# A recurrent attention and maxout kernel: k and v of the first step move to the ScalarE DMA queue

## The chip, the cores and the metric

The kernel runs on one core of a Trainium2 chip. The metric is the device time of one execution in microseconds. A core has five engines that run beside one another and wait for one another by semaphores: TensorE (PE), VectorE (DVE), ScalarE (ACT), GpSimd (POOL) and SyncE (SP). SyncE and ScalarE each have a queue on which they issue DMAs.

## The reference

```
state = alpha[t, :, None] * state + outer(k[t], v[t])     # for each of 4 batches x 8 heads, head width 48
y[t]  = q[t] @ state                                      # t = 0 .. 767
x     = y laid out as 3072 tokens x 384
out   = max(x @ w1, x @ w2, x @ w3) @ w_out               # 384 -> 768 -> 384
```

The inputs q, k, v and alpha are float32 of shape (4, 8, 768, 48), the output is float32, 3072 x 384.

## The kernel before

The sequence is cut into six blocks of 128 positions, and the batches into two pairs; one step is one block of one pair (16 heads), so there are twelve steps. Step s works on block s // 2. Within a block, the recurrence is done as masked attention, after k and q have been scaled by cumulated decays. Between blocks a state is carried.

Each step loads four tiles of 128 positions x 16 heads x 48 values in float32, named ra (alpha), rk, rq and rv; each is one DMA of 384 KB whose rows are 192 bytes. The function `load` (lines 81 to 87) issues them in the order alpha, k, q, v, all on the SyncE queue, and each kind of tile has four buffers. Two constants are loaded on the ScalarE queue: c16 (line 92, 128 x 386 in float16, the triangle, the identity, the mask and a small weight, c_68 in the profile) and c32 (line 93, 128 x 6 in float32, biases and scales of ScalarE's activations, c_69 in the profile). In the program `load(0)` comes first, then the two constants, then `load(1)` and `load(2)`, the twelve loads of weights (lines 120 and 125), `load(3)` and `load(4)`. Later loads are issued one per step. Ahead of everything, ScalarE loads its table of functions (line 72). On each queue the DMAs are issued in program order.

The order of the compute work is written out by hand, in strings of pieces such as `D0@1` (piece D, half 0, step 1), and each engine takes its part of them in that order. The prologue starts with

```
N0@0 H11@0 D0@0 D1@0 H9@0 N0@1 V0@0 T0@0 T1@0 A0@0 A1@0 D0@1 Y0@0 D1@1 T0@1 N0@2 ...
```

- N (`logs`, line 137): ScalarE takes the logarithm of alpha. Its output is a tile la.
- H (`warm`, line 296): TensorE multiplies a blank tile, 512 columns at a time, 11 times or 9 times here. Nothing reads the result.
- D (`decays`, lines 146 to 163): TensorE multiplies the triangle in c16 with the logarithms (L146) and gathers sums (L149). ScalarE takes two exponentials with biases from c32 (ic at L155, ac at L156). VectorE (GpSimd from step 3 on) multiplies k by ic and q by ac (L159, L160).
- V (`values`, line 170): ScalarE scales v with a column of c32. Its output is vt.
- T (`turn`, lines 179 and 183): TensorE transposes the scaled q and k with the identity in c16, VectorE copies them out.
- A (`scores`, lines 193 and 196): scores on TensorE, masked on VectorE.
- Y (`attend`, lines 207 to 214): the attention output on TensorE, copied out by ScalarE (xb, L214). X (`turn_back`, lines 222 and 225) transposes it for the second part.
- W casts weights on GpSimd (L130), M and S carry the state (L233 to L254), G (L268) and O (L285) are the matmuls of the second part.

TensorE, ScalarE and VectorE all work in order, so an instruction that waits holds up what is behind it on its engine. After the prologue, a string FIRST does the second part for steps 0 and 1, and from step 2 on each step runs the attention of a later step beside the second part of an earlier one.

Of the kernel before, what the change touches and what calls it, by code (L numbers as in the profile page):

```python
# [23 lines left out]
def kernel(  # L24
# [12 lines left out]
    nc = tc.nc  # L37
# [40 lines left out]
    def where(s):  # L78
        return s // (B // U), (s % (B // U)) * U

    def load(s):
        cb, b0 = where(s)
        for n in ("a", "k", "q", "v"):
            t = raw.tile([P, NH, D], FP32, name=f"r{n}", tag=f"r{n}")
            nc.sync.dma_start(  # L85
                t, ins[n][cb * P:(cb + 1) * P, b0:b0 + U].rearrange("s b h d -> s (b h) d"))
            raws[s, n] = t

    c16 = cpool.tile([P, 3 * P + 2], FP16, name="c16")
    c32 = cpool.tile([P, 6], FP32, name="c32")  # L90
    load(0)
    nc.scalar.dma_start(c16, nc.inline_tensor(c16_np, name="c16").ap())
    nc.scalar.dma_start(c32, nc.inline_tensor(c32_np, name="c32").ap())
# [240 lines left out]
    LAST = """G0 G1 G2 G3 G4 G5 G6 G7 O1 G8 O0"""  # L334

    load(1)
    load(2)
    load_weights()
    load(3)
# [43 lines left out]
```

## Time and profile before

| What | us |
|---|---|
| time before, median of 2 runs | 171.71 |
| the two runs | 170.89 and 172.54 |
| span of the profiled execution, first to last instruction | 168.8 |
| the median above that span | 2.9 |
| TensorE (matmul) busy, share of the span | 156.9, 93% |
| VectorE busy | 112.2, 66% |
| ScalarE busy | 99.0, 59% |
| GpSimd busy | 49.0, 29% |

For the profiled execution only its span is recorded; how far its own time lies above that isn't recorded apart, so the median stands for it. Times in the profile count from the span's start. In the list of DMA issues, the last number is the time from the issue to the landing of the data. SPq and ACTq are the DMA queues of SyncE and ScalarE, and a busy entry on them is the time that the issue took. The rows with digits cut the span into 40 slices of about 4.2 us, and a 9 means 90% busy or more. In a table of stretches the columns are the stretch, its length, the busy time and count of PE, PEld (the loading of weights into TensorE), DVE, ACT and POOL, the clock granted to TensorE, the mean busy share of the 16 DMA engines (over 1 when their packets overlap), and GB/s.

### The profile page before, as it was taken

What the parts mean: (1) busy time and instruction counts of PE and PEld (TensorE: products, weight loads), DVE (VectorE), ACT (ScalarE), POOL (GpSimd) and SP (SyncE); (2) the same over time, 40 slices, a digit from 0 to 9 for tenths busy, and PEclk for the clock granted to TensorE, in tenths of its full rate; (3) what the DMA queues carried; (4) which work ended last, traced back from release to release, by engine and by line L of the source; (5) the groups of instructions that cost most, each with busy time, mean ns of one, the idle gap of its engine ahead of it and who ended that gap; (6) DMA issues with size and microseconds to landing.
All of it is one profiled execution on the core that took longest, in us unless ns stands there. A gap on an engine that the chain in (4) does not pass through costs nothing.

```text
span 168.8 us, 4329 instructions
## 1 busy us (share of the span) xinstructions
PE 156.9 (93%) x1758; PEld 121.1 (72%) x1758; DVE 112.2 (66%) x185; ACT 99.0 (59%) x181; POOL 49.0 (29%) x72
## 2 busy tenths in 40 slices
PE   7955859999999999999999999999999999999992
PEld 2423637699887676886877978968968869869860
DVE  4186777756647757597587587687667775975730
ACT  3616585142777684874974964956856748435232
POOL 0000005756063454404512531541442244100000
PEclk9995675599999999999999999999999999999999
DMA  6999999998999999999897967948931011020013
GB/s 131 223 219 218 176 247 336 355 360 170 226 172 213 218 248 254 192 226 221 219 223 189 235 105 177 228 91 192 212 92 50 0 56 41 0 93 4 0 47 140
DMA packets 107251, 28.68 MB, mean 170 GB/s; under 512 B 99808, under 2 KB 107232, under 8 KB 107232
## 3 DMA queue, kind: packets, MB, share of 16 engines
q1 hardware_dynamic: 106944, 28.32, 77.3%
q8 instruction: 13, 0.21, 0.6%
q10 hardware_dynamic: 288, 0.10, 0.3%
q14 instruction: 6, 0.05, 0.1%
HBM read 23.69 MB, written 4.72 MB: 168 GB/s over the span
## 4 chain that ended last, share of the span: by engine, by line
PE 81%; SPq 7%; DMA 3%; ACT 3%; DVE 2%; issue 1%; ACTq 0%
PE ops L285 14%; SPq L85 7%; PE tps L179 6%; DMA ra<-in_alpha_dram 3%; PE yps L210 3%; PE xtp L222 2%; PE lps L146 2%; PE yps L207 2%; PE sps L250 2%; PE sps L247 2%; DVE lat L196 1%; PE lps L149 1%; ACT xb L214 1%; PE gps_514 L268 1%; PE gps_523 L268 1%
## 5 line engine op out<-in xcount | busy, mean ns | idle before, releaser
L268 PEld LDWEIGHTS <-wcat 128*128 128x128 f16 x648 | 60.3, 98 | 9.0 <-POOL gm L235 0.2
L285 PE MATMUL ops<-wo_97,hT 128*128 128x384 f16 x144 | 27.1, 327 | 0.0
L288 ACT COPY ob<-ops 128x384 f32<-128x384 f32 x24 | 11.5, 480 | 14.2 <-PE ops L285 14.2
L155 ACT ACTIVATE ic<-lps,c_69 128x384 f32<-128x384 f32 x24 | 13.9, 581 | 8.4 <-PE lps L146 5.1
L285 PEld LDWEIGHTS <-hT 128*128 128x128 f16 x144 | 12.8, 98 | 7.5
L183 DVE COPY qkT<-tps 128x1024 f16<-128x1024 f16 x24 | 16.4, 683 | 1.3 <-PE tps L179 1.1
L214 ACT ACTIVATE xb<-yps,c_69 128x384 f16<-128x384 f32 x24 | 14.0, 585 | 4.8 <-PE yps L210 4.8
L156 ACT ACTIVATE ac<-lps,c_69 128x384 f32<-128x384 f32 x24 | 13.8, 575 | 0.0
L210 PE MATMUL yps<-vt,lat 128*128 128x48 f16 x192 | 12.2, 190 | 0.6 <-ACT vt L170 0.6
L193 PEld LDWEIGHTS <-qkT 48*128 48x128 f16 x192 | 6.3, 98 | 8.8 <-issue 7.7
L159 POOL TENSOR_TENSOR qk_87<-rk,ic 128x384 f16<-128x384 f32 x6 | 6.0, 997 | 21.9 <-ACT ic L155 21.9
L210 PEld LDWEIGHTS <-lat 128*128 128x128 f16 x192 | 10.5, 101 | 1.5 <-DVE lat L196 0.7
L170 ACT ACTIVATE vt<-rv,c_69 128x768 f16<-128x768 f32 x12 | 11.3, 940 | 0.0
L225 ACT COPY xT<-xtp 128x768 f16<-128x768 f16 x12 | 9.6, 803 | 1.0 <-PE xtp L222 1.0
L296 PE MATMUL wps<-blank 128*128 128x512 f16 x22 | 8.0, 528 | 1.2 <-DVE blank L343 1.2
L159 POOL TENSOR_TENSOR qk_86<-rk,ic 128x384 f16<-128x384 f32 x4 | 4.0, 997 | 15.4 <-ACT ic L155 15.4
L130 POOL CAST wcat<-ws_0_114 128x768 f16<-128x768 f32 x1 | 0.8, 823 | 26.3 <-DMA ws_0_114<-in_moe_w_dram 26.3
L159 POOL TENSOR_TENSOR qk_85<-rk,ic 128x384 f16<-128x384 f32 x4 | 4.0, 995 | 13.9 <-ACT ic L155 13.9
L207 PEld LDWEIGHTS <-qkT 128*128 128x128 f16 x80 | 7.7, 98 | 0.4
L222 PE MATMUL xtp<-c_68,xb 128*128 128x128 f16 x72 | 7.4, 228 | 0.5 <-ACT xb L214 0.3
L159 POOL TENSOR_TENSOR qk_84<-rk,ic 128x384 f16<-128x384 f32 x4 | 4.0, 996 | 12.4 <-ACT ic L155 12.4
L222 PEld LDWEIGHTS <-xb 128*128 128x128 f16 x72 | 5.2, 101 | 2.3 <-ACT xb L214 0.9
(409 smaller groups left out, 359.6 us busy)
## 6 DMA issues: line engine op xcount, KB each, us to landing
ra<-in_alpha_dram SPq DMA_DIRECT2D x12, 384.0 KB, 4.7
rk<-in_k_dram SPq DMA_DIRECT2D x12, 384.0 KB, 5.6
rq<-in_q_dram SPq DMA_DIRECT2D x12, 384.0 KB, 5.8
rv<-in_v_dram SPq DMA_DIRECT2D x12, 384.0 KB, 5.7
out_dram<-ob SPq DMA_DIRECT2D x24, 192.0 KB, 2.0
ws_0_114<-in_moe_w_dram SPq DMA_DIRECT2D x1, 384.0 KB, 4.9
ws_1_116<-in_moe_w_dram SPq DMA_DIRECT2D x1, 384.0 KB, 4.5
ws_2_118<-in_moe_w_dram SPq DMA_DIRECT2D x1, 384.0 KB, 5.0
```

The lines of the kernel that those rows point to most:

```text
L85: nc.sync.dma_start(t, ins[n][cb * P:(cb + 1) * P, b0:b0 + U].rearrange("s b h d -> s (b h) d"))
L155: nc.scalar.activation(out=ic, in_=lv, func=AFT.Exp, bias=nat_c, scale=-1.0)
L156: nc.scalar.activation(out=ac, in_=lv, func=AFT.Exp, bias=at_c)
L159: eng.tensor_mul(kv, raws[s, "k"][:, hs], ic)
L170: nc.scalar.mul(vt, raws.pop((s, "v")), vs_c)
L183: nc.vector.tensor_copy(out=qkT, in_=tps)
L210: nc.tensor.matmul(yps[:, p, i, :], lat[:, i, p, :], vt[:, u * H + 2 * p + i, :], start=(cb == 0), stop=(cb == 0 or i == 1))
L214: nc.scalar.mul(xb, yps.rearrange("p a b d -> p (a b d)"), ys_c)
L222: nc.tensor.transpose(xtp[:, u, f, :], xb[:, f * P:(f + 1) * P], ident)
L268: nc.tensor.matmul(gps[:, j, :], wcat[:, f, g, jj * P:(jj + 1) * P], xT[:, f].rearrange("p u t -> p (u t)"), start=(f == 0), stop=(f == NF ...
L285: nc.tensor.matmul(ops, hT_of[s][:, jj, u * P:(u + 1) * P], wo16[:, jj, :], start=(jj == 0), stop=(jj == NJ - 1))
L288: nc.scalar.copy(out=ob, in_=ops)
```

## The change

In step 0, and only there, the loads of k and v are issued on the ScalarE queue. Alpha and q stay on SyncE's. The program order of the four loads and of the constants is unchanged, so ScalarE's queue now holds k, v, c16, c32 and SyncE's holds alpha and q of step 0, then alpha, k, q, v of step 1, and so on. No other instruction moves on any engine.

```
         for n in ("a", "k", "q", "v"):
             t = raw.tile([P, NH, D], FP32, name=f"r{n}", tag=f"r{n}")
-            nc.sync.dma_start(
+            queue = nc.scalar if s == 0 and n in "kv" else nc.sync
+            queue.dma_start(
                 t, ins[n][cb * P:(cb + 1) * P, b0:b0 + U].rearrange("s b h d -> s (b h) d"))
             raws[s, n] = t
```

More of the change, by code (lines that the diff above doesn't have):

```diff
@@ L84, in load @@
             t = raw.tile([P, NH, D], FP32, name=f"r{n}", tag=f"r{n}")
-            nc.sync.dma_start(
+            queue = nc.scalar if s == 0 and n in "kv" else nc.sync
+            queue.dma_start(
                 t, ins[n][cb * P:(cb + 1) * P, b0:b0 + U].rearrange("s b h d -> s (b h) d"))
```

## The prediction

> **What bounds the kernel now.** I read the page first, then the timeline of the first 24 us, the DMA issues with their times to landing, the stretches of 2 us, and the chain that ended last. The page says that TensorE sets the time once it is running:
>
> ```profile
> span 168.8 us, 4329 instructions
> PE   7955859999999999999999999999999999999992
> DMA  6999999998999999999897967948931011020013
> PE 81%; SPq 7%; DMA 3%; ACT 3%; DVE 2%; issue 1%; ACTq 0%
> ```
>
> TensorE is full from slice 8 (about 30 us) to the end; before that it has gaps, and the DMA engines are full from slice 2 to 11. So the change, which touches only the loads of step 0, works in the first 30 us, and what it delays there comes out at the end one for one, unless a gap in the first 30 us takes it up. The timeline of that start:
>
> ```profile
> 0.74 0.43 SPq L85 DMA_DIRECT2D ra<-in_alpha_dram  x1
> 0.77 0.40 ACTq L92 DMA_DIRECT2D c_68<-c  x1
> ...
> 1.20 0.69 ACTq L93 DMA_DIRECT2D c_69<-c  x1
> 1.22 1.42 SPq L85 DMA_DIRECT2D rk<-in_k_dram  x1
> ...
> 5.22 0.84 ACT L137 ACTIVATE la_80<-ra 128x768 f16<-128x768 f32 x1 [3.20 <-DMA ra<-in_alpha_dram]
> ...
> 6.12 0.64 PE L146 MATMUL lps<-la_80,c_68 128*128 128x384 f16 x2
> ...
> 6.64 0.58 ACT L155 ACTIVATE ic<-lps,c_69 128x384 f32<-128x384 f32 x1 [0.57 <-PE lps L146]
> ...
> 6.80 2.10 PE L296 MATMUL wps<-blank 128*128 128x512 f16 x9
> ...
> 9.28 0.62 PE L179 MATMUL tps<-c_68,qk_84 128*128 128x128 f16 x8 [0.38 <-DVE qk_84 L160]
> ```
>
> Three things are to be seen. The ScalarE queue issues c16 (c_68) at 0.77 and c32 (c_69) at 1.20, beside its table load. The first real matmul (L146, 6.12) needs alpha's logarithm and c16's triangle; the first exponential (6.64) needs c32. From there the chain to the first transposes (9.28) has no DMA wait in it. When these transfers land:
>
> ```profile
> rk<-in_k_dram SPq DMA_DIRECT2D x1, 384.0 KB, 5.5
> rq<-in_q_dram SPq DMA_DIRECT2D x1, 384.0 KB, 5.9
> rv<-in_v_dram SPq DMA_DIRECT2D x1, 384.0 KB, 5.8
> ...
> c_68<-c ACTq DMA_DIRECT2D x1, 96.5 KB, 2.9
> c_69<-c ACTq DMA_DIRECT2D x1, 3.0 KB, 3.9
> ```
>
> With the issue times: c16 at 0.77 + 2.9 = 3.7, c32 at 1.20 + 3.9 = 5.1, alpha at 5.2 (its logarithm starts there), k at 6.7, q at 8.6, v at 4.63 + 5.8 = 10.4. One load lands each 1.8 us, and the stretches show why:
>
> ```profile
> 4.00:6.00 2.00, 2.00 (x5) 0.60 (x4) 0.00 (x0) 0.78 (x1) 0.00 (x0) 1.00 1.31 229
> 6.00:8.00 2.00, 1.95 (x17) 1.03 (x16) 0.56 (x1) 1.43 (x4) 0.00 (x0) 1.00 1.35 218
> ```
>
> The last two columns are the DMA share, over 1, and 218 to 229 GB/s. So one load costs 1.75 us of the DMA engines, not of the issuing queue: SyncE's issues take 1.75 us because they wait for room. Last, the chain, where it leaves the loads:
>
> ```profile
> 13.63 5.76 DMA ra<-in_alpha_dram
> ...
> 19.41 0.84 ACT la_82 L137
> ...
> 20.25 0.47 ACT xb L214
> ...
> 20.72 0.83 ACT vt L170
> ```
>
> It makes step 2's alpha look like the bound. But ScalarE's next instruction there, xb, waits for attend matmuls that end at 20.06, and in the trace it starts at 20.16. Without the load it could start at 20.08. The compute chain of steps 0 and 1 thus arrives within 0.1 us of the load, and what shifts it shifts everything.
>
> **What the Trainium skill says.** "DMA: Bandwidth & Descriptors", section "Issuing engines are not separate DMA queues": transfers started by the scalar and the sync engine run on the same 16 DMA engines and interleave; a second issuer saves only issue time. The trace agrees: the DMA share is full with one issuer. The same page, "Queues, rings and completion order": each DMA engine goes round robin between the queues that have work, a packet at a time. The trace agrees as far as it goes: c16, issued after alpha, lands 1.5 us before it. "TensorE: Matmul & The Clock Gate", Part 1: after an idle window of about 3.4 us the clock halves, and it needs as long a busy one to return. Here nine 512-column matmuls take 2.10 us warm, 0.23 each, and the first eleven 4.87 us, 0.44 each; the page's clock row halves at about 13 us, after a thin stretch.
>
> **The change part by part.**
> 1. SyncE loses two issues (k and v of step 0). Its queue is throttled by the engines, and the sum of bytes is the same, so step 1 and step 2's loads land about when they did. Worth 0 to -0.1 us, since the load of step 2 hides at most 0.08 us. Its later waits, for a transfer eight places back, keep their partners (v of step 1 waits for k of step 0, now on ScalarE's queue, long landed).
> 2. Alpha and k now start together (0.74 and about 0.77) and share the engines packet by packet. Both land when k did, less the share of the constants that were ahead: about 6.5. Alpha is 1.3 us later.
> 3. The constants stand behind k and v in ScalarE's queue. When that queue has moved k and v, round robin has moved alpha and q on the other: all four loads, as much as was moved when v landed before. So c16 lands at about 10.4, not 3.7, and c32 0.1 to 1.4 us later (it was 1.4 later before): about 11.
> 4. ScalarE's own logarithm is behind two long issues. Room is some 1.5 loads per queue (SyncE's third issue ends at 4.59, when 1.5 loads have gone); v's issue, then the constants', should end by 5 to 7.5, and the logarithm after them by 8.4 at the latest: hidden behind c16.
> 5. So L146 goes from 6.12 to about 10.5, +4.4. The first exponential follows with it or with c32: +4.4 to +5.2. VectorE then has the operands of the transposes at 13.7 to 14.5.
> 6. TensorE is idle from 6.06 (end of the eleven warm matmuls) to 10.5, 4.4 us, longer than the clock's window: it restarts at half clock. The decays' matmuls then take 1.0 instead of 0.7 us, and the nine warm matmuls, in order ahead of the transposes, 9 x 0.43 = 3.9 instead of 2.1. They end at 15.3 if the clock stays down, 14.3 if it returns midway. Before they were hidden (0.38 us idle before the transposes); now they end last. Transposes at 14.3 to 15.3 instead of 9.28: +5.0 to +6.0; with c32's share I take +5.5.
> 7. From there VectorE and ScalarE set the pace by latency as before, with k, q and v of step 1 (14.0 to 17.6) now long landed. Step 2's alpha (19.4) is no longer waited for: -0.1. The weights land at the same times, and their casts have 5 us more room; nothing is gained, as TensorE did not wait for them.
> 8. The dense part begins at half clock (its first two groups of six matmuls take 1.39 and 1.28 us, later ones 0.66), about 1.6 us in all. A start 5 us later falls otherwise on the clock's windows: -1 to +1, taken as 0.
>
> Sum: +5.4 us. On the profiled span: 168.8 + 5.4 = 174.2. The median of the two runs stands 2.9 us above that span, for what lies around it, so 171.7 + 5.4 = **177.1 us**, taken as 177.0 (+3.1%). Within this account the bounds are +3 (c16 at 9.0, TensorE still warm) and +8 (c32 at 12, cold throughout, the dense part +1).
>
> **The rivals.**
> - A: two rings move more, or ScalarE's is preferred. For: weights with longer rows move at 355 GB/s, so the engines aren't at their limit in bytes. Against: a share over 1 with short rows. At 355 GB/s the four loads and c16 (1.67 MB) need 4.7 us from the first byte at 1.95, plus the 1.2 us that alpha took from last byte to landing: 7.9. L146 is 1.8 later, TensorE stays warm: 173.5.
> - B: SyncE's ring is preferred, so alpha and k of step 1 pass ahead of the constants, 1.75 to 3.5 us more: c16 at 12 to 14, +7 to +9: 180.
> - C, not slower: the loads of step 2 are the bound, as the chain shows them, and two issues fewer ahead of them bring them earlier while step 0's delay stays in the idle time (ScalarE waits 3.5 us for step 1's alpha and 1.7 for step 2's). Price: -0.1 us, 171.6; more only if step 0 starts earlier as well. It decides if c16 lands by 6.2. That needs 1.67 MB in about 3.1 us, 540 GB/s, where no slice exceeds 360; or ScalarE's ring served wholly first, and then alpha is late instead. TensorE's order also puts step 1 behind all of step 0.
>
> **How the numbers follow.** Forecast 0.75, A 0.13, B 0.08, C 0.04. The range, 173.8 to 179.6, takes the account's bounds and a part of A and B. Two per cent is 3.4 us, about what a measurement of this kernel tells from no change (its two runs differ by 1.0%). Within it lie A, half of C and the lowest 0.03 of the forecast: 0.18; faster 0.02; slower 0.80.
>
> **What would show it.** Right: c16 lands near 10.4 from ScalarE's queue, alpha near 6.5; L146 starts near 10.5 with idle time ahead of it; the nine warm matmuls near 0.43 each; first transposes at 14.3 to 15.3; no wait for step 2's alpha; TensorE full from about 35.5. Wrong: c16 below 8, alpha still at 5.2, a DMA rate well above 230 GB/s in the first 8 us, or a later wait that takes up the shift before 35 us.

## The result, and the profile after

| | before | after |
|---|---|---|
| time, median of 2 runs | 171.71 us | 178.06 us (177.83 and 178.30) |
| span of the profiled execution | 168.8 us | 175.9 us |

The ratio is 1.040, with a 95% interval of 1.028 to 1.052: slower, by 6.35 us between the medians and by 7.1 us between the profiled spans. (The profiled execution before is among the shorter of its kind, so the two differences needn't agree.) In the experiments below the time is the median of all of a kernel's runs, but the ratio and its interval are of its fast runs alone, those within about 1.5% of its fastest, so that one run of 384 us of the kernel before and one of 523 us with the constants between k and v don't count in it. After the edit the line numbers of the profile are one higher from line 86 on.

The page of the changed kernel:

```profile
span 175.9 us, 4328 instructions
PE   7329477789999999999999999999999999999992
DMA  6999999999999839999489793993972001010013
PE 83%; DMA 5%; DVE 4%; ACT 3%; ACTq 1%; issue 1%
```

TensorE now has a hole in slices 2 and 3 (4.4 to 13 us), at 3 and 2 tenths where it was at 9 and 5 before. From slice 11 on it is as full as it was. The DMA engines are full from slice 2, as before. The chain that ended last no longer leads back through SyncE's issues (7% before), but through one DMA of a constant. Its pieces of the start, longest at the constant:

```profile
1.28 2.08 ACTq L86
...
3.39 8.60 DMA c<-c
...
12.04 0.82 PE lps L147 x2
...
13.05 3.86 PE wps L297 x9
16.92 0.67 PE tps L180 x8
```

c16 is issued at 3.39, when ScalarE's queue has got rid of v, and lands 8.6 us later, at 12.0. The decays' matmul follows at once, then the nine warm matmuls at 3.86 us, then the first transposes. The timeline of the same stretch, with what waited:

```profile
0.76 0.48 ACTq L86 DMA_DIRECT2D rk<-in_k_dram  x1
...
1.28 2.08 ACTq L86 DMA_DIRECT2D rv<-in_v_dram  x1
...
3.39 4.13 ACTq L93 DMA_DIRECT2D c<-c  x1
...
7.55 0.46 ACTq L94 DMA_DIRECT2D c<-c  x1
8.05 0.84 ACT L138 ACTIVATE la<-ra 128x768 f16<-128x768 f32 x1 [6.04 <-issue]
...
12.04 0.82 PE L147 MATMUL lps<-la,c 128*128 128x384 f16 x2 [5.98 <-DMA c<-c]
...
12.92 4.00 PE L297 MATMUL wps<-blank 128*128 128x512 f16 x9
...
16.71 1.31 PE L180 MATMUL tps<-c,qk 128*128 128x128 f16 x16
```

The decays start 5.9 us later than before (12.04 against 6.12), the transposes 7.4 later (16.71 against 9.28), and the dense part, the first group of matmuls of the second part of the kernel, 7.3 later (37.80 against 30.51). Its first line before, and after:

```profile
30.51 1.46 PE L268 MATMUL gps_514<-xT,wcat 128*128 128x256 f16 x6
```

```profile
37.80 2.74 PE L269 MATMUL gps<-xT,wcat 128*128 128x256 f16 x12
```

The span is 7.1 longer. So the delay that stands at the first transposes is what comes out at the end.

When the transfers land, from the DMA issues of the first 8.5 us (the last column is the time to landing):

```profile
rk<-in_k_dram ACTq DMA_DIRECT2D x1, 384.0 KB, 5.5
rq<-in_q_dram SPq DMA_DIRECT2D x1, 384.0 KB, 7.2
rv<-in_v_dram ACTq DMA_DIRECT2D x1, 384.0 KB, 8.6
...
c<-c ACTq DMA_DIRECT2D x1, 96.5 KB, 8.6
c<-c ACTq DMA_DIRECT2D x1, 3.0 KB, 4.7
```

With the issue times, k lands at 6.3, q at 8.4, v at 9.9, c16 at 12.0 and c32 at 12.3. Alpha of step 0 lands at 0.74 + 4.7 = 5.4, alpha of step 1 at 2.60 + 9.0 = 11.6, ahead of c16. ScalarE's logarithm, behind the long issues of v and c16, is held up to 8.05, but it is done 3 us before c16 lands. Which queue moved packets when, by the packets of each in four stretches (3 to 4, 5.3 to 6.7, 7.5 to 8.5 and 9 to 10.5 us; q1 is SyncE's queue, q10 ScalarE's; packets, MB, share of 16 engines):

```profile
q1 hardware_dynamic: 676, 0.13, 63.8%
q10 hardware_dynamic: 680, 0.13, 63.8%
```

```profile
q1 hardware_dynamic: 1541, 0.30, 137.1%
q10 hardware_dynamic: 56, 0.01, 4.4%
```

```profile
q10 hardware_dynamic: 1133, 0.22, 140.5%
q1 hardware_dynamic: 13, 0.00, 1.5%
```

```profile
q1 hardware_dynamic: 1683, 0.32, 138.9%
q10 hardware_dynamic: 19, 0.00, 1.8%
```

Only in the first stretch do the two queues share packet by packet. After it one queue is served at a time, each for about a whole load: q, then v, then alpha of step 1. c16, a small transfer behind v, waits for a whole load of the other queue. The rate is no higher with two queues: 218 or 219 GB/s in each of the last three stretches, against 218 before.

### The profile page after: what moved, and what is told of

Read it like the earlier page. It is cut to its first block, busy times and chain, and to the rows that moved or that the text cites. A ratio compares the mean times of both kernels' runs of the same rounds, so it can differ in the third digit from the quotient of the medians.

```text
span 175.9 us, 4328 instructions
## 1 busy us (share of the span) xinstructions
PE 158.7 (90%) x1758; PEld 121.8 (69%) x1758; DVE 112.0 (64%) x185; ACT 99.0 (56%) x181; POOL 48.9 (28%) x72
## 4 chain that ended last, share of the span: by engine, by line
PE 83%; DMA 5%; DVE 4%; ACT 3%; ACTq 1%; issue 1%
PE gps L269 41%; PE ops L286 14%; PE tps L180 7%; PE aps L194 5%; DMA c<-c 5%; PE lps L147 3%; PE yps L211 3%; PE wps L297 3%; PE xtp L223 3%; DVE lat L197 2%; PE yps L208 2%; PE sps L251 2%; PE sps L248 1%; ACTq L86 1%; DVE qkT L184 1%; PE lps L150 1%
## 5 line engine op out<-in xcount | busy, mean ns | idle before, releaser
L269 PE MATMUL gps<-xT,wcat 128*128 128x256 f16 x648 | 82.9, 275 | 0.0
L279 DVE TENSOR_TENSOR h<-gps,h 128x512 f16<-128x512 f32 x36 | 24.9, 692 | 23.3 <-PE gps L269 19.8
L160 POOL TENSOR_TENSOR qk<-rk,ic 128x384 f16<-128x384 f32 x18 | 18.0, 1001 | 71.3 <-ACT ic L156 71.3
L277 ACT CAST h<-gps 128x512 f16<-128x512 f32 x36 | 21.1, 587 | 29.4 <-PE gps L269 29.0
L197 DVE TENSOR_TENSOR lat<-aps,c 128x512 f16<-128x512 f32 x48 | 30.8, 685 | 7.8 <-PE aps L194 7.8
L279 DVE TENSOR_TENSOR hT<-gps,h 128x512 f16<-128x512 f32 x36 | 24.9, 692 | 10.7 <-PE gps L269 9.0
L286 PE MATMUL ops<-wo,hT 128*128 128x384 f16 x144 | 27.1, 327 | 0.0
L289 ACT COPY ob<-ops 128x384 f32<-128x384 f32 x24 | 11.6, 482 | 14.1 <-PE ops L286 14.1
L161 POOL TENSOR_TENSOR qk<-rq,ac 128x384 f16<-128x384 f32 x18 | 18.0, 999 | 0.0
L180 PE MATMUL tps<-c,qk 128*128 128x128 f16 x192 | 16.0, 233 | 2.1 <-DVE qk L161 1.7
L215 ACT ACTIVATE xb<-yps,c 128x384 f16<-128x384 f32 x24 | 14.1, 587 | 6.5 <-PE yps L211 6.5
L138 ACT ACTIVATE la<-ra 128x768 f16<-128x768 f32 x12 | 10.2, 853 | 6.0 <-issue 6.0
```

The costliest lines, as they stand in the source:

```text
L160: eng.tensor_mul(kv, raws[s, "k"][:, hs], ic)
L161: eng.tensor_mul(qv, raws[s, "q"][:, hs], ac)
L180: nc.tensor.transpose(tps[:, i, p, :], qk[:, i, u * HP + p].rearrange("p a b -> p (a b)"), ident)
L197: nc.vector.tensor_mul(lat[:, i], aps[i], mask.unsqueeze(1).broadcast_to([P, HP, P]))
L215: nc.scalar.mul(xb, yps.rearrange("p a b d -> p (a b d)"), ys_c)
L269: nc.tensor.matmul(gps[:, j, :], wcat[:, f, g, jj * P:(jj + 1) * P], xT[:, f].rearrange("p u t -> p (u t)"), start=(f == 0), stop=(f == NF ...
```

## The experiments

Theory 1: the loss is the constants' place behind k and v. Theory 2, its rival: the loss comes of large loads on ScalarE's queue as such, through the shared engines and ScalarE's own logarithm behind the issues. All times are compared with the kernel before on the same chip: 171.49 us for the constants first, the constants last, only v moved, and all warm matmuls ahead; 171.21 for the other three.

**The constants first.** The two loads stay on ScalarE's queue, and the constants go ahead of them.

```
-    load(0)
     nc.scalar.dma_start(c16, ...)
     nc.scalar.dma_start(c32, ...)
+    load(0)
```

> The changed kernel, with the two constants issued on ScalarE's queue ahead of k and v. Theory 1, the loss is the constants' place behind k and v: c16 lands again near 3.7, L147 starts after alpha's logarithm, by 6.1 to 7.5, the transposes by 9.3 to 10.7, and the time is 171 to 173.5, within 1% of before. Theory 2, the loss is that two large loads are on ScalarE's queue at all (they share the engines with alpha, and their issues hold ScalarE's logarithm up to about 8): L147 not before 8.9, the transposes from 12 on, the time 174 to 177.

Measured: 171.51 us, ratio 1.000 (0.996 to 1.005). The timeline:

```profile
0.76 0.40 ACTq L92 DMA_DIRECT2D c<-c  x1
...
5.38 0.84 ACT L138 ACTIVATE la<-ra 128x768 f16<-128x768 f32 x1 [3.37 <-DMA ra<-in_alpha_dram]
...
6.28 0.48 PE L147 MATMUL lps<-la,c 128*128 128x384 f16 x2 [0.82 <-ACT la L138]
...
9.68 0.62 PE L180 MATMUL tps<-c,qk 128*128 128x128 f16 x8 [0.78 <-DVE qk L161]
```

c16 lands at 0.76 + 2.7 = 3.5, ScalarE's logarithm isn't held up (5.38), the decays start at 6.28, and the whole loss is gone, with k and v still on ScalarE's queue. Theory 2 falls. The same run says what moving the loads is worth when nothing stands in its way: nothing that this measurement can tell.

**The constants last, all on SyncE's queue.** The kernel before, with the constants behind its four loads and nothing on ScalarE's queue.

```
     load(0)
-    nc.scalar.dma_start(c16, ...)
-    nc.scalar.dma_start(c32, ...)
+    nc.sync.dma_start(c16, ...)
+    nc.sync.dma_start(c32, ...)
```

> The kernel before, with the two constants issued on SyncE's queue behind a, k, q and v of step 0; ScalarE's queue carries nothing. Theory 1, the constants' place alone costs the time: c16 lands at about 10.8 (behind v at 10.4), L146 near 10.9, nine slow warm matmuls, transposes near 15.6, time 176.5 to 178. Theory 2, the use of ScalarE's queue costs it: alpha lands before 5.2, nothing is shared, time 171 to 173.

Measured: 175.46 us, ratio 1.025 (1.017 to 1.033). The timeline:

```profile
4.38 0.84 ACT L137 ACTIVATE la<-ra 128x768 f16<-128x768 f32 x1 [2.36 <-DMA ra<-in_alpha_dram]
...
5.94 1.64 SPq L92 DMA_DIRECT2D c<-c  x1
...
10.10 0.82 PE L146 MATMUL lps<-la,c 128*128 128x384 f16 x2 [5.03 <-DMA c<-c]
```

The place alone costs some 60% of it by the ratios (2.5% of 4.0%; 1.7% to 3.3% by the interval), without a load on ScalarE's queue and with alpha 0.8 us earlier. It is a little below the expected 176.5: c16 lands at 10.0 and not 10.8, and in the profiled run the dense part begins at full clock (its first twelve matmuls take 1.48 us, against 2.74 before and in the changed kernel), so that the transposes are 5.2 us late (14.47) and the span only 3.7 longer. On one queue c16 comes 0.4 us after v (4.08 + 5.6 = 9.7), on two queues 2.1 us after it (12.0 against 9.9).

**Only v moved.** k goes back to SyncE's queue, so the constants stand behind one load.

```
-            queue = nc.scalar if s == 0 and n in "kv" else nc.sync
+            queue = nc.scalar if s == 0 and n == "v" else nc.sync
```

> The changed kernel with only v on ScalarE's queue, k back on SyncE's: the constants stand behind one load and not two. Theory 1 with an even share of the two queues: c16 lands when v and one load of SyncE's have moved, about 6.7; L147 at 6.8 to 7.5, TensorE still warm, time 172.5 to 174. Theory 1 with SyncE's queue served ahead, as the changed kernel's trace suggests (c16 landed after step 1's alpha, at 12.0): c16 at 8 to 9, L147 +2 to +3, the warm matmuls in part slow, time 174 to 175.5. Theory 2 (ScalarE's queue as such): as the changed kernel, 177 to 178.

Measured: 174.47 us, ratio 1.020 (1.013 to 1.028). c16, issued at 1.28, lands at 8.3, 2.0 us behind v (0.76 + 5.5 = 6.3); the decays wait for it, and the transposes start at 12.24:

```profile
8.30 0.82 PE L147 MATMUL lps<-la,c 128*128 128x384 f16 x2 [2.86 <-DMA c<-c]
```

This is the answer expected of a queue that isn't shared evenly: with even shares c16 would have landed at 6.7. The loss grows with how late c16 lands: none at 3.5, 3.0 us at 8.3, 4.0 at 10.0 (all on SyncE's queue), 6.35 at 12.0.

**The constants between k and v.** This tests whether the queues take turns.

```
         for n in ("a", "k", "q", "v"):
             ...
+            if s == 0 and n == "k":
+                constants()        # the two DMAs of c16 and c32, no longer behind load(0)
```

> The changed kernel with the two constants issued on ScalarE's queue between k and v. Theory of turns, after the first pair of loads the two queues take turns transfer by transfer: the order is alpha and k, q, c16, so c16 lands just after q, at 8.3 to 8.9, L147 at 8.4 to 9.2, the warm matmuls mostly slow, time 174 to 175.5. Theory of an even share, packet by packet: c16 right behind k, at 6.5 to 6.9, L147 by 7.2, time 172 to 173.5.

Measured: 174.86 us, ratio 1.022 (1.009 to 1.034). The packets of 5.5 to 6.5 us, with SyncE's queue alone, and of 6.5 to 7.5, with the constants in it:

```profile
q1 hardware_dynamic: 1135, 0.22, 141.9%
```

```profile
q1 hardware_dynamic: 584, 0.11, 73.2%
q10 hardware_dynamic: 251, 0.11, 55.2%
```

c16 lands at 1.27 + 6.9 = 8.2 beside q (8.7), 1.9 us behind k (6.3). The even share's 6.5 to 6.9 is excluded, and c16 fits turns of whole transfers but for 0.1 us. But v, behind the constants on ScalarE's queue, doesn't fit them. Its issue and that of step 1's alpha on SyncE's queue, and their times to landing:

```profile
2.59 3.31 SPq L86 DMA_DIRECT2D ra<-in_alpha_dram  x1
...
3.94 0.46 ACTq L86 DMA_DIRECT2D rv<-in_v_dram  x1
```

```profile
ra<-in_alpha_dram SPq DMA_DIRECT2D x1, 384.0 KB, 9.5
rv<-in_v_dram ACTq DMA_DIRECT2D x1, 384.0 KB, 6.3
```

v lands at 10.2 and this alpha at 12.1, where strict turns would have moved alpha between the constants and v. What fits is the end of the issues: v's ended at 4.40, alpha's at 5.90. In every trace here with loads on both queues, the loads issued in the first 10 us landed in the order in which their issues ended, whichever queue they stood on, and c16, where it was behind a load, landed within 0.6 us of the load whose issue had ended last before its own. (With the constants first, k, issued after q but with an issue that ended at 2.21 against 3.35, landed at 7.2 against 8.9.) This was read from the traces afterwards; no run was made to test it.

The warm matmuls were not slow, as expected, but took 2.10 us, after 2.2 us without work for TensorE. The transposes came only 1.4 us later than before (10.71), the dense part 2.6 later (33.12): here the delay at the transposes isn't all that comes out at the end.

**The changed kernel again**, on the chip of the run above and of the last one below.

> The changed kernel again, to stand on the same chip as the next two. All theories: 177 to 178.5, the first transposes at 16.5 to 16.8 (15.7 to 16.8 if the clock returns midway).

Measured: 177.61 us, ratio 1.041 (1.034 to 1.049); transposes at 16.68, dense part from 37.58.

**All warm matmuls ahead.** Thirty ahead of the decays, none behind.

```
-    N0@0 H11@0 D0@0 D1@0 H9@0 N0@1 ...
+    N0@0 H30@0 D0@0 D1@0 N0@1 ...
```

> The changed kernel with the warm matmuls in one group of 30 ahead of the decays, and none between the decays and the transposes. If the slow clock after the idle time is a cost of its own: no idle time over 2.5 us ahead of L147 at 12.0, the transposes no longer wait for warm matmuls but for VectorE, at 15.1 to 15.3 instead of 16.7, and the time is 1.4 to 1.7 lower than the changed kernel's. If the warm matmuls only fill time that is lost anyway (VectorE would be late too): transposes at 16.5 or later, time unchanged within 0.5.

Measured: 176.90 us, ratio 1.031 (1.024 to 1.038), against 1.040 and 1.041 for the changed kernel, about the gain that was expected, but the intervals overlap. The transposes start at 14.14, 2.6 earlier than in the changed kernel, more than expected. But the dense part starts at 37.02, only 0.8 earlier. The stretches show where it went (the eleventh number on a line, the third from the right, is TensorE's clock):

```profile
12.00:14.00 2.00, 0.68 (x10) 0.46 (x10) 0.94 (x2) 1.56 (x4) 0.00 (x0) 0.92 1.34 214
14.00:16.00 2.00, 1.85 (x16) 1.54 (x16) 1.72 (x4) 2.00 (x4) 0.00 (x0) 0.50 1.38 221
```

TensorE has little to do between 12 and 14, and its clock halves just as the transposes begin.

**Thirty ahead and the nine kept.** The nine fill that stretch.

```
-    N0@0 H11@0 D0@0 D1@0 H9@0 N0@1 ...
+    N0@0 H30@0 D0@0 D1@0 H9@0 N0@1 ...
```

> The changed kernel with 30 warm matmuls ahead of the decays and the nine after them kept. If the gain of the run with the 30 alone (transposes 2.6 earlier) was lost again because the clock fell soon after: here the nine run at full clock (2.0 to 2.2 in all), transposes at 14.7 to 15.1, the clock stays up for the scores, and the dense part starts 1.5 or more ahead of the changed kernel's 37.8; time 1.5 to 2 lower than the changed kernel's. If the later clock is set by the thin stretch from 16 on, whatever is done before: dense part at 36.9 to 37.4, time 0.5 to 1 lower.

Measured: 175.94 us, ratio 1.023 (1.011 to 1.036), 1.7 us below the changed kernel between the medians and about 3.1 by the ratios (1.023 against 1.041). The dense part starts at 35.45, 2.1 earlier than in the changed kernel on that chip. Timeline and one stretch:

```profile
12.48 2.10 PE L297 MATMUL wps<-blank 128*128 128x512 f16 x9
...
14.42 1.16 PE L180 MATMUL tps<-c,qk 128*128 128x128 f16 x16
```

```profile
34.00:36.00 2.00, 1.55 (x21) 1.21 (x19) 2.00 (x5) 0.52 (x1) 1.56 (x2) 0.95 1.08 358
```

So the slow clock is a cost of its own: of the 7.4 us at the transposes, 16.7 - 14.4 = 2.3 were the nine matmuls at half clock and what they held up. The intervals of these two runs and the changed kernel overlap, so this rests on the traces rather than on the times. In the profiled run the dense part also starts at full clock, which the changed kernel's does not; how much of that is owed to the edit and how much to chance stays open, as it is so with the constants last too, where no warm matmuls were added.

## Why the prediction was right

The forecast was 177.0 us and slower; measured were 178.06. Its mechanism is shown in both directions: with the constants ahead the loss is gone (1.000), and with the constants behind the loads on one queue alone it is there (1.025). By its steps:

1. SyncE's two issues fewer bring nothing. Right: step 2's alpha lands at 13.52 + 5.8 = 19.3, as before. Nothing waits for it any more (its logarithm runs at 24.90), so rival C, that the loads of step 2 are the bound, falls.
2. Alpha and k sharing evenly and both landing at 6.5. Wrong: alpha lands at 5.4 and k at 6.3, so alpha is only 0.2 us late. The share was even for one load, and in it alpha was ahead.
3. c16 at 10.4. This is the term that was mis-sized: it landed at 12.0. The step took the two queues to be served evenly, packet by packet, all along. After the first pair the loads were moved nearly whole, one after the other, and step 1's alpha, whose issue ended at 5.91, went ahead of c16, whose issue ended at 7.52. This is what rival B priced, at its lower end, but not for B's reason: SyncE's queue isn't preferred, as v ahead of step 1's alpha shows in the run with the constants between k and v. Whether the engines left the round robin, or had work of one queue only at a time, isn't shown. c32 at 11 became 12.3, and hid behind the slow decays, as the exponential's wait shows (12.58, after the matmul).
4. ScalarE's logarithm behind its issues. Right in kind: it ran at 8.05 to 8.89, a little past the bound of 8.4, hidden behind c16.
5. The decays at +4.4. Measured +5.9, by step 3.
6. The slow clock. Right: the nine matmuls took 4.00 us, 0.44 each, and ended last ahead of the transposes. The clock did not return midway in the profiled run, so the transposes stood at +7.4 and not at +5.0 to +6.0.
7. From there nothing is gained back. Right within 0.1 us: 7.4 at the transposes, 7.3 at the dense part.
8. The dense part's clock taken as 0. Right here, by chance: its first twelve matmuls took 2.74 us, half clock as before, and the full clock came 3.3 us after the dense part began in both. Over the other profiled runs it came between 3.1 and 4.3 us after the beginning, or before it (constants last; thirty and the nine). By an estimate, half the slow time, that is worth up to about 2 us of the span.

The sum was 5.4 for a measured 7.1 on the profiled span. Most of the difference is c16's 1.6 us. Against the medians it was 5.4 for 6.35, and it came closer by luck: the median stood 2.9 us above the profiled span before, but only 2.2 after.

One reading of the kernel before was at fault without harm. The text says that the chain from 6.12 to the transposes has no DMA wait. VectorE's second multiply there starts at 8.66, while ac was ready at 7.7 and q landed at 8.6: it waited for q, though the view names ScalarE. With the constants first, where q lands at 1.23 + 7.7 = 8.9, the transposes start at 9.68 and not 9.28.

## What to carry to other kernels

When transfers move to another queue, look at what already stands on that queue and at who waits for it first: a small constant behind two large loads cost more than the loads could gain. The DMA engines were full, so a second queue brought no bandwidth (the Trainium skill, "DMA: Bandwidth & Descriptors", section "Issuing engines are not separate DMA queues", says that a second issuer saves only issue time, and the run with the constants first agrees, at 1.000); it changed only the order, and the order has to follow the order of need. If TensorE then idles at the start, count the slow clock afterwards as well (here 4.00 us for nine matmuls that take 2.10).

## What the runs showed of the hardware that was not expected

In the changed kernel, two queues with large loads of 192-byte rows shared the engines packet by packet only while the first pair was moved; then about one transfer of 2048 packets was moved at a time (1541 to 56 packets, then 13 to 1133, then 1683 to 19). In every trace here with loads on both queues, the loads of this start landed in the order in which their issues ended, on whichever queue. A transfer of 96.5 KB behind another on its own queue then landed 1.9 to 2.1 us after it, against 0.4 us when one queue held everything. The issue of this small transfer itself lasted 4.1 us on ScalarE's queue, behind two loads, and held ScalarE's logarithm up from 5.4, when alpha had landed, to 8.05. Why the transfers are moved in this way wasn't settled.
